# Two weight loads moved ahead of a branch, and a decode moved one step later, in a routed expert and gated block on one core

## The chip, the cores and the metric

The kernel runs on one core of a Trainium2 chip. The metric is the device time of one execution in microseconds, taken as the median of three runs. The profile is one execution of the same program, recorded by the hardware profiler; its rows count time from the first instruction.

## The reference

Linear attention, a routed expert layer and a gated linear block follow one another. All data is float32, but the weights of the gated block and of the router may arrive as 64-bit words, which the kernel decodes itself.

```python
kv  = einsum('bhsd,bhse->bhde', k, v)                 # 8 x 8 heads, 576 tokens, 64 wide
out = einsum('bhsd,bhde->bhse', q, kv)
x   = out / rms(out) * g_norm                         # 4608 tokens x 512
e   = argmax(x @ w_gate + modality_bias[modality_id]) # one of 8 experts
x   = gate_w * (relu(x @ w1[e]) @ w2[e])              # 512 -> 1024 -> 512, per token's expert
y   = (sigmoid(x @ wg) * (x @ wv)) @ wo               # 512 -> 1536 -> 512
```

## The kernel before

Every product is made of bfloat-like halves: an operand is split by ScalarE (ACT) into a rounded high part, and by VectorE (DVE) into the rest, and TensorE (PE) makes three matmuls of the halves. All order is written out by hand; each engine runs its instructions in the order of the program. The sync engine (SP) issues nearly all transfers, from one queue that runs in order: an instruction that has to wait holds all behind it.

The expert part handles 26 items, each in four steps. The last four sure items (`NSURE - 4` on) also carry work for the gated block, placed by `later(q, do)` at step q of the last 16. They load and transpose the first block of 512 tokens, load the weight rows of steps 0 and 1 of the gated block (`rows[0]`, `rows[1]`, 128 x 4 x 256 each, 512 KB) at q = 2, and split them: `split0` reads `rows[0]` at q = 8 and 10, `split1` reads `rows[1]` at q = 13 and 14 and stores the halves to `wt_d`. Then step 0 of the gated block is computed (`gv_first`), and a branch follows (`tc.If`): the items that are only sometimes needed are skipped or run.

Behind the branch the gated block runs over 5 blocks of tokens (the first of 512, the others of 1024) times 12 columns of 128 of the inner width: steps s = 1 to 59 (`NU` = 60). Steps 1 to 11 belong to the first block (`glu_plain`): 12 matmuls for the gate, then 12 of the output product of the step before, then 12 for the value. While PE does these, `prepare(s, spot)` is called at eight spots, in the order 0, 1, 6, 7, 2, 5, 4, 3, where 0 stands before the first product and 2 to 3 behind the second.

- Spot 0 issues loads: the output rows `wo` (`load_raw`, L922), `load_rows(s + 2)` (L1290) into `rows[s % 2]`, and a raw unit (`decode_late`, L1646).
- Spots 1 and 2 split the rows of step s + 1 (`group`: ACT L972, DVE L973); spot 2 also stores the halves (L1316).
- Spot 4 splits the output rows of step s + 1 (L1345, L1346) and the product of step s (L1350, L1351), which DVE has just multiplied (L996); it also scales the tokens of the next block by their gate (`weigh_y`, ACT L942, with factors that an indirect load fetches, L938) where a table (`TURNS`) says so.
- Spot 3 transposes such tokens on PE (L947), copies them out, and decodes a raw unit (`decode_late2`).

A unit is a 128 x 512 block of a weight, 512 KB as 64-bit words. Of 36 units 28 are decoded in the expert part. The last eight (`Late`, units 0 to 7) are decoded in the gated block: one ACT instruction (L1651), five DVE instructions (L1655 to L1661), and a store of 256 KB to `w_d` (L155 for units 0 to 3, L157 for units 4 to 7). Units 0 to 3 are the last four blocks of the value weight, which the rows of steps 8 to 11 need; units 4 to 7 are the output rows of steps 8 to 11. Two raw buffers alternate. Before, units 0 and 1 are loaded ahead of step 1, unit s in step s (2 to 7), and unit s - 1 is decoded at the end of step s (1 to 8). The tile `late` that holds them is handed on by `hold_y` at step 9, for split tokens of the next block.

Of the kernel before, what the change touches and what calls it, by code (L numbers as in the profile page):

```python
# [84 lines left out]
def attention_moe_glu_kernel(  # L85
# [4 lines left out]
    nc = tc.nc  # L90
# [825 lines left out]
    rows = [y0p.tile([128, 4, 256], F32, name=f"rows{i}") for i in range(2)]  # L916
# [3 lines left out]
    def load_raw(s, k):  # L920
        raw_o[s, 0] = (y0p if k % 2 == 0 else late_pool[0]).tile([128, DM], F32, tag="wo", name="wo", bufs=1)
        nc.sync.dma_start(out=raw_o[s, 0], in_=w_d[k // 4][:, k % 4, 1024:1536])  # L922
# [44 lines left out]
    def w_rows(j):  # L967
        return w_d[j // 4][:, j % 4, 0:1024].rearrange("p (k f) -> p k f", f=256)

    def split_w2(src, dst):  # L970

        nc.scalar.activation(out=dst[:, :, 0, :], in_=src, func=ACTF.Copy)  # L972
        nc.vector.tensor_tensor(out=dst[:, :, 1, :], in0=src, in1=dst[:, :, 0, :], op=ALU.subtract)  # L973
# [74 lines left out]
    with ExitStack() as st:  # L1048
# [12 lines left out]
        jobs = {}  # L1061
# [27 lines left out]
        def later(q, do):  # L1089
            tail.setdefault((NSURE - 4 + q // NJ1, q % NJ1), []).append(do)  # L1090
# [14 lines left out]
        def split0(g):  # L1105
            wt_first.append(dec.tile([128, 2, 2, 256], F32R, tag="d_raw", name="d_raw", bufs=4))
            split_w2(rows[0][:, 2 * g:2 * g + 2], wt_first[g])
            if g == 0:
                nc.sync.dma_start(out=wt_d[0][:, 0:2], in_=wt_first[0].bitcast(F32))
            else:  # L1110
                nc.sync.dma_start(out=wt_d[0][:, 2:3], in_=wt_first[1][:, 0:1].bitcast(F32))

        def split1(g):
            if g == 0:
                wts.append(grp.tile([128, 7, 2, 256], F32R, name="wt1"))
            split_w2(rows[1][:, 2 * g:2 * g + 2], wts[0][:, 2 * g:2 * g + 2])
            if g:
                nc.sync.dma_start(out=wt_d[1][:, 0:3], in_=wts[0][:, 0:3].bitcast(F32))
# [10 lines left out]
        for g in range(2):  # L1129
            later(8 + 2 * g, lambda g=g: split0(g))  # L1130
            later(13 + g, lambda g=g: split1(g))

        def gv_first(at):
            bank = lambda n: (phh.tile([128, 512], F32, tag="ph", name="ph") if n == "a" else
                              ptx.tile([128, 512], F32, tag="xt", name="xtp"))
            tmp = lambda n: xp.tile([128, XW], F32, tag="xg", name="xg", bufs=4)[:, 0:HC]
            glu_plain(lambda k: wt_first[k // 2][:, k % 2], y_of0, bank, tmp, lambda h: gm0, at)
# [73 lines left out]
    with ExitStack() as st:  # L1211
# [76 lines left out]
        def load_rows(s):  # L1288
            if s < 2 * NJ:
                nc.sync.dma_start(out=rows[s % 2], in_=w_rows(s % NJ))  # L1290

        def load_wt(s):
            if NJ <= s < NU:
                n = 3 if s < 2 * NJ else 7
                for lo, hi in ((0, 1), (1, n)):
                    nc.sync.dma_start(out=wts[s % 2][:, lo:hi].bitcast(F32), in_=wt_d[s % NJ][:, lo:hi])
# [3 lines left out]
        def sum_w(s):  # L1300


            if NJ <= s < 2 * NJ:
                r = rows[s % 2]
                t = wsum[s] = ws.tile([128, 4, 256], F32, tag="wsum", name="wsum", bufs=1)
                add = lambda o, a, c, op: nc.vector.tensor_tensor(out=o, in0=a, in1=c, op=op)
                add(t[:, 0], r[:, 3], r[:, 2], ALU.add)
                add(t[:, 1], t[:, 0], r[:, 0], ALU.subtract)
                add(t[:, 2], r[:, 0], r[:, 3], ALU.subtract)
                add(t[:, 3], r[:, 1], t[:, 1], ALU.subtract)  # L1310

        def group(s, g):
            if s < NJ:
                split_w2(rows[s % 2][:, 2 * g:2 * g + 2], wts[s % 2][:, 2 * g:2 * g + 2])
                if g:
                    nc.sync.dma_start(out=wt_d[s][:, 0:3], in_=wts[s % 2][:, 0:3].bitcast(F32))  # L1316
            elif s < 2 * NJ:
                a = 3 + 2 * g
                split_w2(wsum[s][:, 2 * g:2 * g + 2], wts[s % 2][:, a:a + 2])
                if g:  # L1320
                    nc.sync.dma_start(out=wt_d[s % NJ][:, 3:7], in_=wts[s % 2][:, 3:7].bitcast(F32))
# [6 lines left out]
        def load_o(s, z):  # L1328
            if (s, z) not in step_at:
                return  # L1330
            b, h, k = step_at[s, z]
            if b:
                split_o[s, z] = new_wos()
                nc.sync.dma_start(out=split_o[s, z].bitcast(F32), in_=wo_d[k][:, :, :])

        def ready_o(s, z):


            if (s, z) not in step_at:
                return  # L1340
            b, h, k = step_at[s, z]
            if b == 0:
                src = raw_o.pop((s, z))
                t = split_o[s, z] = new_wos()
                nc.scalar.activation(out=t[:, 0], in_=src, func=ACTF.Copy)  # L1345
                nc.vector.tensor_tensor(out=t[:, 1], in0=src, in1=t[:, 0], op=ALU.subtract)  # L1346
                nc.sync.dma_start(out=wo_d[k][:, :, :], in_=t.bitcast(F32))
            src = gms.pop((12 * b + k, h))
            hi, lo = (ws.tile([128, HC], F32R, tag=t, name=t, bufs=3) for t in ("gh", "gl"))
            nc.scalar.activation(out=hi, in_=src, func=ACTF.Copy)  # L1350
            nc.vector.tensor_tensor(out=lo, in0=src, in1=hi, op=ALU.subtract)  # L1351
            split_g[s, z] = (hi, lo)
            free_g.append(src)
# [261 lines left out]
        def number_y(b, i):  # L1615
            number(b, i, yr[i])
# [17 lines left out]
        jobs = {}  # L1634
# [27 lines left out]

        def decode_late(s):

            for i in ((0, 1) if s == 0 else (s,) if 1 < s < 8 else ()):
                jobs[i] = Late(units[NEARLY + i], i)

        def decode_late2(s):
            if 1 <= s < 9:
                d = jobs.pop(s - 1)  # L1670
                d.exponent()
                d.words()
                d.finish()
                d.store()

        def prepare(s, spot):


            b, j = divmod(s, NJ)
            if spot == 0:  # L1680
                load_wt(s + 1)
                if s + 2 <= NJ:
                    load_raw(s + 2, s + 1)
                load_rows(s + 2)
                decode_late(s)
                sum_w(s + 1)
            if spot == 6:
                ready_o(s, 1)
                load_o(s + 1, 0)
                load_o(s + 1, 1)  # L1690
            if spot == 1:
                group(s + 1, 0)
            if spot == 7:
                out_step((s, 0))
            if spot == 2:
                group(s + 1, 1)
            if spot == 4:
                ready_o(s + 1, 0)
                out_step((s, 1))
            if s > OPEN:  # L1700
                chunk_step(s, spot)
            if b + 1 < NB:
                for what, do in TURNS[min(b, 1)].get((j, spot), ()):
                    what(b + 1, do)
                if s == 9 and spot == 0:
                    hold_y(mw[1].tile([128, 2, 2, 2, HC], F32R, tag="w2r1", name="w2r1"))
                if s == 11 and spot == 3:
                    hold_y(yA[0][:, 0:2])
                if b and j == NJ - 1 and spot:
                    free_y.append(Y.pop((b, spot)))  # L1710
                for what in YPLAN[min(b, 2)].get((j, spot), ""):
                    y_step(b + 1, what)
            if b > 1:
                for what in YPLAN[min(b - 1, 2)].get((j + NJ, spot), ""):
                    y_step(b, what)
            if spot == 3:
                decode_late2(s)
            sums_o(s, spot)
            if (s, spot) == (FIRST, 0):
                yslots.extend(xp.tile([128, XW], F32, tag="xg", name="yr", bufs=4) for _ in range(2))  # L1720
                free_g.extend(xp.tile([128, XW], F32, tag="xg", name="yr", bufs=4)[:, 0:HC] for _ in range(2))
            if s == NU - 1 and spot in SPOTS[1:7]:
                last_load(SPOTS.index(spot) - 1)
            if (s, spot) == (OPEN, 3):
                open_chunks()
                chunk_step(s, spot)
# [2 lines left out]
        tmp = lambda n: ws.tile([128, HC], F32, tag=n, name=n, bufs=1)  # L1729
        late_pool.append(ws)  # L1730
        load_raw(2, 1)
        load_rows(2)
        for i in range(4):
            load_y(1, i)
        for i in range(4):
            number_y(1, i)
        decode_late(0)
        ready_o(1, 0)
        hold_y(yA[0], 2)
        hold_y(mw[1].tile([128, 2, 2, 2, HC], F32R, tag="w1r1", name="w1r1"))  # L1740
# [47 lines left out]
```

## Time and profile before

| | |
|---|---|
| median of 3 runs | 1472.84 us (1471.26 to 1475.34) |
| the profiled execution | 1472.33 us, of which its span (first to last instruction) 1470.5 us |
| granted TensorE clock, mean | 0.992 of full speed |
| busy, share of the span | PE 96%, DVE 69%, ACT 46%, POOL 18% |
| moved by DMA | 365.34 MB, mean 248 GB/s |

A busy share is the time in which the engine executes anything. PE's busy time counts pipelined matmuls whose ends are modelled, so 96% is not 96% of its peak. The clock column of the windows shows which of its two levels PE was granted: 1.00 is 2.4 GHz, 0.50 is 1.2 GHz.

### The profile page before, as it was taken

How to read it: one execution, taken by the hardware profiler on the slowest of the kernel's cores; microseconds unless marked ns; L12 is line 12 of the kernel's file. 1: busy time of each engine (PE TensorE's matmuls, PEld its weight loads, DVE VectorE, ACT ScalarE, POOL GpSimd, SP SyncE). 2: the span in 40 equal slices, each digit the busy share in tenths (PEclk: the TensorE clock that was granted, in tenths of full speed). 3: DMA queues.
4: the chain of work that ended last, by engine and by line, in shares of the span. 5: the costliest groups of instructions: out<-in, count | busy, mean ns of one | idle time of the engine just before them, and what ended most of it. 6: DMA issues, size and time to landing. Idle time of an engine off the chain costs nothing.

```text
span 1470.5 us, 24842 instructions
## 1 busy us (share of the span) xinstructions
PE 1417.6 (96%) x9302; PEld 1240.9 (84%) x9302; DVE 1009.5 (69%) x1592; ACT 677.6 (46%) x1080; POOL 269.7 (18%) x356
## 2 busy tenths in 40 slices
PE   6997999999999999989999999999999999999996
PEld 6886789999999998778888887888889888898896
DVE  1567868888888877647866676565876468655574
ACT  3676555556555556746433342332433235222241
POOL 1021122223121213111011101011024200131025
PEclk9999999999999999999999999999999999999999
DMA  9987599998985857689887656886666655565553
GB/s 297 332 302 248 184 318 309 267 327 284 302 287 187 289 164 241 235 273 335 317 337 255 243 194 248 327 285 232 208 215 221 207 203 186 196 215 199 193 162 111
DMA packets 189708, 365.34 MB, mean 248 GB/s; under 512 B 22544, under 2 KB 114448, under 8 KB 182416
## 3 DMA queue, kind: packets, MB, share of 16 engines
q1 hardware_dynamic: 177408, 330.37, 66.8%
q0 software_dynamic: 10816, 32.08, 6.0%
q8 instruction: 75, 1.23, 0.3%
q10 hardware_dynamic: 1360, 1.26, 0.3%
q14 instruction: 49, 0.40, 0.1%
HBM read 301.31 MB, written 74.93 MB: 256 GB/s over the span
## 4 chain that ended last, share of the span: by engine, by line
PE 52%; DMA 2%; DVE 1%; POOL 1%; issue 1%; ACT 0%; SPq 0%; another core or an unknown queue 0%; POOLq 0%; ACTq 0%; DVEq 0%
PE gv L1010 10%; PE gv L1011 10%; PE gv L1012 10%; PE ac L1490 4%; PE ac L1488 3%; PE ac L1489 3%; PE ac L1382 2%; PE ac L1383 2%; PE ac L1384 2%; PE gv L984 1%; PE gv L986 1%; PE gv L985 1%; PE tr L947 1%; DMA wos<-wp_d 1%; DMA rows<-w_d 1%
## 5 line engine op out<-in xcount | busy, mean ns | idle before, releaser
L279 PE MATMUL ph<-xh,w1h 128*128 128x256 f32 x576 | 167.2, 290 | 1.1 <-ACT w1h L235 1.1
L280 PE MATMUL ph<-xh,w1l 128*128 128x256 f32 x576 | 163.5, 284 | 0.9 <-DVE w1l L237 0.9
L281 PE MATMUL ph<-xl,w1h 128*128 128x256 f32 x576 | 163.5, 284 | 0.0
L1014 DVE TENSOR_TENSOR u<-u,gv 128x512 f32<-128x512 f32 x144 | 98.5, 684 | 78.5 <-PE gv L1012 77.8
L1488 PE MATMUL ac<-wos,gh 128*128 128x256 f32 x480 | 135.7, 283 | 2.3 <-ACT gh L1457 1.1
L1490 PE MATMUL ac<-wos,gl 128*128 128x256 f32 x480 | 136.3, 284 | 1.4 <-DVE gl L1450 1.3
L1489 PE MATMUL ac<-wos,gh 128*128 128x256 f32 x480 | 135.9, 283 | 0.0
L1010 PE MATMUL gv<-half,wt 128*128 128x512 f32 x336 | 132.2, 393 | 0.0
L1011 PE MATMUL gv<-half,wt 128*128 128x512 f32 x336 | 131.3, 391 | 0.0
L1012 PE MATMUL gv<-half,wt 128*128 128x512 f32 x336 | 131.0, 390 | 0.0
L279 PEld LDWEIGHTS ph<-xh,w1h 128*128 128x128 f32 x576 | 110.8, 192 | 3.0 <-ACT w1h L235 1.3
L280 PEld LDWEIGHTS ph<-xh,w1l 128*128 128x128 f32 x576 | 110.9, 193 | 2.8 <-DVE w1l L237 1.1
L281 PEld LDWEIGHTS ph<-xl,w1h 128*128 128x128 f32 x576 | 110.6, 192 | 0.0
L335 PE MATMUL py<-w2h,hh 128*128 128x512 f32 x272 | 106.9, 393 | 0.0
L336 PE MATMUL py<-w2l,hh 128*128 128x512 f32 x272 | 106.8, 393 | 0.0
L337 PE MATMUL py<-w2h,hl 128*128 128x512 f32 x272 | 106.0, 390 | 0.0
L1488 PEld LDWEIGHTS ac<-wos,gh 128*128 128x128 f32 x480 | 91.8, 191 | 7.2 <-issue 1.4
L1489 PEld LDWEIGHTS ac<-wos,gh 128*128 128x128 f32 x480 | 91.8, 191 | 3.7
L1490 PEld LDWEIGHTS ac<-wos,gl 128*128 128x128 f32 x480 | 91.8, 191 | 1.9 <-DVE gl L1450 1.8
L349 POOL DMA_INDIRECT y_d<-y,sidx x36 | 40.4, 1122 | 283.2 <-ACT y L345 110.5
L1043 ACT ACTIVATE u<-u 128x512 f32<-128x512 f32 x48 | 30.4, 633 | 134.1 <-DVE u L1014 134.1
L301 ACT ACTIVATE hh<-ph 128x512 fp32r<-128x512 f32 x68 | 40.6, 598 | 105.5 <-PE ph L281 105.5
(408 smaller groups left out, 3736.1 us busy)
## 6 DMA issues: line engine op xcount, KB each, us to landing
wt<-wt_d SPq DMA_DIRECT2D x36, 1536.0 KB
half<-in_moe_w_dram SPq DMA_DIRECT2D x96, 512.0 KB
w1r<-in_moe_w_dram SPq DMA_DIRECT2D x40, 512.0 KB
w2r<-in_moe_w_dram SPq DMA_DIRECT2D x40, 512.0 KB
wos<-wp_d SPq DMA_DIRECT2D x72, 256.0 KB
rows<-w_d SPq DMA_DIRECT2D x24, 512.0 KB
wt<-wt_d SPq DMA_DIRECT2D x48, 256.0 KB
wt_d<-wt SPq DMA_DIRECT2D x12, 1024.0 KB
```

Source lines behind the costliest of these rows:

```text
L279: nc.tensor.matmul(out=o, lhsT=bh[:, c, cs], rhs=hi[:, c, 0:n], start=(c == 0), stop=False)
L280: nc.tensor.matmul(out=o, lhsT=bl[:, c, cs], rhs=hi[:, c, 0:n], start=False, stop=False)
L281: nc.tensor.matmul(out=o, lhsT=bh[:, c, cs], rhs=lo[:, c, 0:n], start=False, stop=(c == KC - 1))
L335: nc.tensor.matmul(out=o, lhsT=hi[:, f, cs], rhs=bh[:, f, :], start=first, stop=False)
L336: nc.tensor.matmul(out=o, lhsT=hi[:, f, cs], rhs=bl[:, f, :], start=False, stop=False)
L337: nc.tensor.matmul(out=o, lhsT=lo[:, f, cs], rhs=bh[:, f, :], start=False, stop=last)
L1010: nc.tensor.matmul(out=o, lhsT=wh, rhs=yh[:, c, :], start=first and c == 0, stop=False, skip_group_check=True)
L1011: nc.tensor.matmul(out=o, lhsT=wh, rhs=yl[:, c, :], start=False, stop=False, skip_group_check=True)
L1012: nc.tensor.matmul(out=o, lhsT=wl, rhs=yh[:, c, :], start=False, stop=last and c == 1, skip_group_check=True)
L1488: nc.tensor.matmul(out=o, lhsT=gh[:, cs], rhs=wh, start=fresh and i % 2 == 0, stop=False, skip_group_check=True)
L1489: nc.tensor.matmul(out=o, lhsT=gh[:, cs], rhs=wl, start=False, stop=False, skip_group_check=True)
L1490: nc.tensor.matmul(out=o, lhsT=gl[:, cs], rhs=wh, start=False, stop=stop, skip_group_check=True)
```

## The change

Four places change. The rows of steps 2 and 3 are loaded ahead of the branch, at q = 12 and q = 15, into the buffers that the splits of steps 0 and 1 have read; the loads of the same rows behind the branch go away. Raw units 0 and 1 are loaded in spot 0 of step 1 instead of ahead of it, that is behind the tokens, the output rows of step 3 and the first store of output halves; unit s - 1 is loaded in step s (3 to 8). Each unit is decoded one step later (steps 2 to 9), and the tile is handed on at step 10.

```diff
@@ expert part, the last 16 steps
         for g in range(2):
             later(8 + 2 * g, lambda g=g: split0(g))
             later(13 + g, lambda g=g: split1(g))
+            later(12 + 3 * g, lambda g=g: nc.sync.dma_start(out=rows[g], in_=w_rows(2 + g)))
@@ gated block
         def decode_late(s):
-            for i in ((0, 1) if s == 0 else (s,) if 1 < s < 8 else ()):
+            for i in ((0, 1) if s == 1 else (s - 1,) if 2 < s < 9 else ()):
                 jobs[i] = Late(units[NEARLY + i], i)
         def decode_late2(s):
-            if 1 <= s < 9:
-                d = jobs.pop(s - 1)
+            if 2 <= s < 10:
+                d = jobs.pop(s - 2)
                 d.exponent()
                 d.words()
                 d.finish()
                 d.store()
@@ prepare, spot 0
                 load_wt(s + 1)
                 if s + 2 <= NJ:
                     load_raw(s + 2, s + 1)
-                load_rows(s + 2)
+                if s > 1:
+                    load_rows(s + 2)
                 decode_late(s)
                 sum_w(s + 1)
@@ prepare
-                if s == 9 and spot == 0:
+                if s == 10 and spot == 0:
                     hold_y(mw[1].tile([128, 2, 2, 2, HC], F32R, tag="w2r1", name="w2r1"))
@@ ahead of step 1
         load_raw(2, 1)
-        load_rows(2)
         for i in range(4):
             load_y(1, i)
         for i in range(4):
             number_y(1, i)
-        decode_late(0)
         ready_o(1, 0)
```

## Rows read from the trace of the kernel before

**Rows 1.** Chain that ended last, behind the branch: start us, us, what.

```profile
637.08 9.04 DMA rows<-w_d
646.21 0.64 ACT wt L972
...
647.48 0.69 DVE gm L996
...
648.73 0.71 ACT yr L942
649.49 1.97 PE tr L947 x8
651.46 0.43 PE gv L984
...
660.25 0.87 PE tr L947 x8
```

**Rows 2.** Waits of PE, 615 to 725 us: total, times, longest us.

```profile
PE tr L947 <- ACT yr L942: 3.8, 1, 3.8
```

**Rows 3.** Windows of PE: us, busy (count), granted clock, DMA share, GB/s.

```profile
53.00:54.00 1.00, 0.72 (x18) 1.00 1.04 389
...
650.00:651.00 1.00, 1.00 (x6) 0.50 0.90 252
...
653.00:654.00 1.00, 1.00 (x6) 1.00 1.01 422
```

**Rows 4.** Timeline of PE near 53 us: start, us, what, idle before.

```profile
53.28 0.73 PE L479 MATMUL kv<-vt,kt 64*64 64x64 f32 x17 [2.70 <-issue]
```

**Rows 5.** Timeline of the SP queue, behind the branch: when a transfer was issued.

```profile
630.15 0.42 SPq L1290 DMA_DIRECT2D rows<-w_d  x1
...
685.04 0.32 SPq L157 DMA_DIRECT2D w_d<-w2r  x1
...
685.89 0.44 SPq L1290 DMA_DIRECT2D rows<-w_d  x1
...
694.09 0.32 SPq L157 DMA_DIRECT2D w_d<-w2r  x1
...
694.94 0.44 SPq L1290 DMA_DIRECT2D rows<-w_d  x1
```

**Rows 6.** Timeline of ACT: its waits for rows in steps 1, 7 and 8.

```profile
634.60 1.15 ACT L972 ACTIVATE wt<-rows 128x512 fp32r<-128x512 f32 x2 [1.89 <-DMA rows<-w_d]
...
692.48 1.15 ACT L972 ACTIVATE wt<-rows 128x512 fp32r<-128x512 f32 x2 [1.60 <-DMA rows<-w_d]
...
701.76 1.16 ACT L972 ACTIVATE wt<-rows 128x512 fp32r<-128x512 f32 x2 [2.78 <-DMA rows<-w_d]
```

**Rows 7.** Timeline of PE: last product of step 2, first of steps 8 and 9.

```profile
645.29 0.39 PE L986 MATMUL gv<-half,wt 128*128 128x512 f32 x1
...
695.40 0.39 PE L984 MATMUL gv<-half,wt 128*128 128x512 f32 x1
...
703.56 0.39 PE L984 MATMUL gv<-half,wt 128*128 128x512 f32 x1
```

**Rows 8.** DMA issues of the page: count, KB each, median us to landing.

```profile
y_d<-y POOLq DMA_DIRECT2D x4, 264.0 KB, 3.5
```

**Rows 9.** Chain that ended last, near the end of the span.

```profile
1424.68 4.41 DMA wos<-wp_d
```

**Rows 10.** Waits of the SP queue, 575 to 725 us.

```profile
SPq L157 <- DVE w2r L1661: 18.7, 4, 5.2
...
SPq L1099 <- DMA y_d<-y,sidx: 8.9, 1, 8.9
```

**Rows 11.** Windows of all engines, shortly before the branch.

```profile
616.00:620.00 4.00, 4.00 (x24) 2.84 (x23) 3.83 (x6) 3.16 (x6) 0.00 (x0) 1.00 0.00 0
```

**Rows 12.** The tile of the scale factors, 635 to 650 us.

```profile
L938 POOL DMA_INDIRECT gate_t<-gate_d,oid x4: 963/980/1376, 636.9 to 641.8; - x4
...
DMA to landing us min/median/max: 5.7/5.8/6.6
```

## The prediction

> **What bounds the kernel now.** I read the page's shares first, then the waits of the matrix engine (PE) around the branch, the chain of waits there, the PE clock, and last the timelines of the sync engine's DMA queue, of ScalarE (ACT) and of PE. PE is busy 96% of the span, so only an idle PE counts, and an edit off PE is worth what it gives or takes there. The table of PE's waits from 615 to 725 us, which holds the end of the expert part, the branch and steps 1 to 11 of the last part, has one wait of size: 3.8 us in which transposes wait for a scaling pass on ACT [rows 2]. PE passes the branch itself almost without a pause. In the chain [rows 1] the reader sees why: the rows load that is issued at 637.08 lands 9.04 us later; only then can ACT split it (646.21); the vector multiply of step 2 (VectorE, DVE) stands behind a split too and starts at 647.48; ACT's split of that product and its scaling of `yr` (648.73) follow; PE starts at 649.49. PE's last product before began at 645.29 and took 0.39 [rows 7], so the idle time is 645.68 to 649.49, 3.81 us. After it the granted clock is 0.50 (1.2 GHz) until it is back at 1.00 (2.4 GHz) by 653 [rows 3]: eight transposes take 1.97 instead of 0.87, and three products 0.43 each instead of 0.23 [rows 1], 1.10 + 0.60 = 1.7 us. So rows that come late cost 5.5 us, 0.37% of the time. That is all the change can win here.
>
> **The change, part by part: the two early rows.** Two rows loads (steps 2 and 3, 512 KB each) leave the queue behind the branch and go before it. No instruction is added. The cover: from 616 to 620, shortly before the branch, the DMA share is 0.00 [rows 11]. The first load goes out when the splits of step 0's rows have freed its buffer, the second behind the store of step 1's split, the last thing that the queue issues before the branch. A 512 KB load needed 4.4 us behind the branch (issued 630.15, ACT released at 634.60, [rows 5, 6]) and at worst 9.04 [rows 1]; the rows are first split in steps 1 and 2, behind the branch, so I cost the two loads at nothing. Were that cover gone, they would cost what they do now.
>
> **Where that stall goes.** With the rows there, ACT and DVE have no split left to do when PE ends step 2. What is late next is a chain of engines that the edit does not touch: multiply on DVE, then ACT's split of it, then ACT's scaling, then PE. From 647.48 to 649.49 that chain takes 2.01 [rows 1]; with 0.05 for the first hand-over PE still idles 2.06. ACT works in program order, so the scaling can't pass the split. The scale factors come by indirect DMA: the four are issued from 636.9 to 641.8 and land 5.7 to 6.6 us later [rows 12]; the two that count are the first two, the second of them issued a third of the way, near 638.5, and in place by 645.1, before ACT comes to them at 647. The gap shrinks by 3.81 - 2.06 = 1.75. Does the clock hold through 2.06 us? An idle time of 2.70 us at 53.28 [rows 4] left it at 1.00 [rows 3], so I take the 1.7 as won too: gain 3.4. Ends: 1.7 (the clock falls all the same) and 5.5 (no gap at all).
>
> **The raw units one step later.** Eight raw loads, eight decodes (one ACT, five DVE instructions) and eight stores remain, each one step later. Early, this only empties the queue: step 1 loads two raw units behind its own inputs, step 2 loads none and stores none. The price is at the other end. The store of a decoded unit is issued as the last act of a step's vector work; the queue waits for it (18.7 us in 4 waits, [rows 10]). Before, every load that reads a decoded piece came a step after its store. Now it comes right behind it: in step 6 the rows of step 8 need unit 3, in steps 7 to 10 the wo load needs units 4 to 7. Such a load can't be issued until the store has landed, and the queue runs in order, so the rows load behind it, the raw load and the stores wait too. That a queue stands still for a landing store is seen elsewhere: 8.9 us for a `y_d` store [rows 10].
>
> Cost of one such wait. Let W be the time from the store's issue to its landing, R that of the rows load. For step 7: the store goes at 694.09 [rows 5], then W, 0.45 for the wo load's issue, R, then the ACT split (0.64) and the DVE one (0.69, as the passes in [rows 1]), and PE wants the result at 703.56 when step 9 starts [rows 7]. Room: 703.56 - 694.09 - 0.45 - 1.33 = 7.69 for W + R. For step 6, whose wo load needs no wait: 695.40 - 685.04 - 1.33 = 9.03.
> W is not in the trace of before. Nearest rows: 3.5 for a 264 KB store from another queue [rows 8], and 4.41 for a 256 KB load on this one [rows 9]; the upper bound is what a rows load takes in the same traffic, 6.8 (694.94 to 701.76, [rows 5, 6]). I take 4.4, nearest in size and queue. R is at least 4.4 (at 630.15, little in front) and at most 6.8; step 6 shows 6.6 (685.89 to 692.48). While the queue waits nothing new is issued, so the traffic in front is smaller than now, but a raw load and two stores follow at once: I take 5.0, near the quiet end. W + R = 9.4, 1.7 over the room of step 7 and 0.4 over that of step 6. Each load serves the step after next, so two chains alternate: step 9 starts 1.7 late, step 11 another 1.7; the chain through steps 8 and 10 gives 0.4 + 1.7, less than the other and covered by it. Sum 3.4. Behind step 10's wait stands the first load of the next phase's weights (step 12); no row says if it is late: between 0 and another 1.7, I take 0.4, as two steps lie between. Loss 3.8. By the lower ends (7.9) it is 2 x 0.2 = 0.4, by the upper ends (13.6) 2 x 5.9 = 11.8.
>
> The Trainium skill (DMA: Bandwidth & Descriptors, section Anatomy of one DMA) says that a DMA engine never waits for a semaphore, the issuing sequencer does; that is the mechanism which speaks against this edit, and the 8.9 us agree. It also gives a fixed cost of some 2.0 us, mostly the write's receipt, plus bytes at 436 GB/s: an estimate of 2.6 for W and 3.2 for R, together 5.8. By it no step is late and the loss is nothing; the measured 3.5 and 4.4 are longer.
>
> The buffer that is handed over at step 10 instead of 9 is first written by an ACT split at the start of step 11. It may wait for the last store by some 2 us; ACT then still does its step-11 sigmoid well before the multiply at that step's end needs it. Cost nothing; without that cover, those 2 us.
>
> **Sum.** -3.4 + 3.8 = +0.4 on the profiled execution's 1472.33 (span 1470.5): 1472.7. The median of the three runs is 0.51 above that execution: 1473.2.
>
> **Rivals.**
> No late step: W + R fits in 7.7. Then only the gain remains, -3.4: 1469.4. For it: the lower ends miss by 0.2 only, and the queue is drained while it waits. Against: ACT already waits 1.60 and 2.78 us for rows [rows 6]. The Trainium skill's figures, by the estimate above, give this case too.
> Slower: the store waits behind a full queue. One mechanism: each step's raw load and two stores go out just before the next decode's store, so W becomes 5.0 (the 4.4 and 0.6 of the traffic in front) and R its worst, 6.8. W + R = 11.8, 4.1 over; twice is 8.2, and one of those idle times, over 3.8, costs the clock again, 1.7. +9.9 - 3.4 = +6.5: 1479.3. It decides from W + R of about 11.6 without a clock fall (2 x 3.9 = 7.8 = 3.4 + 4.4). For it: 6.6 and 6.8 are what R is now. Against: the queue stands empty part of the time.
> Gap wholly gone and no loss: -5.5, 1467.3. For it: the whole idle time is laid to the rows load. Against: the 2.01 us chain of three engines.
> The gap stays because a scale factor or the wo load is late instead: 0 + 3.8, 1476.6. Against: both land before 646 by the rows.
>
> **Chances and range.** Forecast 0.42, no late step 0.22, slower 0.24, gap gone 0.09, gap stays 0.03. Faster or slower by over 0.3% (4.4 us, about what a measurement of this kernel can tell) are only "gap gone", 0.09, and "slower", 0.24; the rest is 0.67. The range goes from just under the no-late-step case to just over the slower one, 1468.9 to 1480: it leaves out the gap-gone case and the worst of W + R. The forecast's own range is 1470 to 1476.
>
> **What would show it.** Right: PE's wait near 645 is about 2 us, and the clock stays at 1.00 at 650; ACT's splits of steps 2 and 3 wait for no DMA; waits of the queue for a `w_d` store appear in steps 6 to 10, 3.5 to 6 us each; PE idles 1 to 2 us at steps 9 and 11. Wrong: no such PE waits between 690 and 730 (then 1469), or PE waits of 3 us and more with the clock at 0.50 after them (then 1479).

## The result, and the profile after

The changed kernel takes 1484.54 us (median of 5; 1481.37 to 1490.22) against 1472.82 (median of 5): ratio 1.0076, 95% interval 1.0061 to 1.0092. It is 11.7 us slower, and 4.5 us above the top of the predicted range.

The profiled execution is the slowest of the five (1490.22 us, span 1488.4), 17.9 us longer than the one shown of before. PE's first product of step 1 starts at 633.42 instead of 629.11, its first of step 12 at 743.16 instead of 728.04. So 4.3 us were lost ahead of the branch, 10.8 between steps 1 and 12 (109.74 us instead of 98.93), and 2.8 behind. The 4.3 are not the change. PE is already 4.3 us later than before at 215 us, some 390 us ahead of the first instruction that moved; and two kernels below whose code is the same up to the branch, rows_alone and rows_weigh, start step 1 at 633.37 and 627.70. Windows of PE in this execution (us, busy, granted clock, DMA share, GB/s) show half clock in work that is the same in both kernels; the execution of before has 1.00 in all three.

```profile
52.00:56.00 4.00, 3.47 (x28) 0.60 1.07 371
93.00:97.00 4.00, 4.00 (x96) 0.60 1.09 358
196.00:199.00 3.00, 2.51 (x11) 0.53 1.05 382
```

Where PE waits, 600 to 780 us, answering to [rows 2]:

```profile
PE gv L984 <- ACT wt L972: 4.6, 2, 3.6
PE gv L1010 <- DMA wt<-wt_d: 2.9, 1, 2.9
PE tr L947 <- ACT yr L942: 2.1, 1, 2.1
```

The old wait is down from 3.8 to 2.1, and two kinds are new: products that wait for split rows, and the first product of the next phase that waits for its weights. PE's timeline (start, us, idle before) gives their places: behind step 2, then steps 9, 10 and 12.

```profile
652.04 1.27 PE L947 MATMUL tr<-ident,yr 128*128 128x128 f32 x8 [2.05 <-ACT yr L942]
...
707.65 0.50 PE L984 MATMUL gv<-half,wt 128*128 128x512 f32 x1 [1.00 <-ACT wt L972]
...
719.93 0.80 PE L984 MATMUL gv<-half,wt 128*128 128x512 f32 x1 [3.56 <-ACT wt L972]
...
743.16 0.79 PE L1010 MATMUL gv<-half,wt 128*128 128x512 f32 x1 [2.92 <-DMA wt<-wt_d]
```

Behind three of the four the granted clock is at its lower level (windows of PE, compare [rows 3]):

```profile
654.00:655.00 1.00, 1.00 (x4) 0.50 0.98 404
...
720.00:722.00 2.00, 2.00 (x5) 0.50 1.00 416
...
746.00:748.00 2.00, 2.00 (x6) 0.50 0.96 389
```

What the products wait for is seen on ACT, whose waits for rows grew from the 1.60 and 2.78 of [rows 6]:

```profile
696.48 1.16 ACT L972 ACTIVATE wt<-rows 128x512 fp32r<-128x512 f32 x2 [2.69 <-DMA rows<-w_d]
...
706.97 1.15 ACT L972 ACTIVATE wt<-rows 128x512 fp32r<-128x512 f32 x2 [5.06 <-DMA rows<-w_d]
...
719.25 1.15 ACT L972 ACTIVATE wt<-rows 128x512 fp32r<-128x512 f32 x2 [7.62 <-DMA rows<-w_d]
```

And what the rows wait for is on the SP queue. Its table of waits, 575 to 740 us, has two rows that before does not have:

```profile
SPq L922 <- DMA w_d<-w2r: 24.5, 4, 7.4
...
SPq L1291 <- DMA w_d<-w2r: 2.7, 1, 2.7
```

Five times the queue stands still until a store of a decoded unit has landed. The SP timeline of steps 7 to 9 (when each transfer was issued) answers to [rows 5]:

```profile
697.02 0.32 SPq L157 DMA_DIRECT2D w_d<-w2r  x1
701.99 0.32 SPq L922 DMA_DIRECT2D wo<-w_d  x1
702.36 0.42 SPq L1291 DMA_DIRECT2D rows<-w_d  x1
702.88 0.38 SPq L1647 DMA_DIRECT2D w2r<-in_moe_w_out_dram  x1
703.35 0.38 SPq L1317 DMA_DIRECT2D wt_d<-wt  x1
703.83 0.51 SPq L1348 DMA_DIRECT2D wo_d<-wos  x1
705.16 0.32 SPq L157 DMA_DIRECT2D w_d<-w2r  x1
712.98 0.32 SPq L922 DMA_DIRECT2D wo<-w_d  x1
713.35 1.50 SPq L1291 DMA_DIRECT2D rows<-w_d  x1
...
716.37 0.83 SPq L157 DMA_DIRECT2D w_d<-w2r  x1
724.44 0.32 SPq L922 DMA_DIRECT2D wo<-w_d  x1
724.80 0.43 SPq L1291 DMA_DIRECT2D rows<-w_d  x1
```

From a store (L157) to the wo load that reads what it wrote (L922) there are 4.97, 7.82 and 8.07 us; in before there are 0.4 (694.09 to 694.50). Read the six lines from 701.99 to 705.16: once released, the queue sends off in 3 us all that it had held back, 2.6 MB in five transfers (256, 512, 512, 768 and 512 KB), and the next store follows straight behind them. From 702 to 713 us, between the release and the landing of that next store, the windows show 262 GB/s, 2.88 MB: the five transfers and the store's own 0.26 MB. So the store landed when all that was sent off ahead of it had been moved.

### The profile page after: what moved, and what is told of

Same layout as the page of the kernel before. It is cut to its first block, busy times and chain, and to the rows that moved or that the text cites. A ratio compares the mean times of both kernels' runs of the same rounds, so it can differ in the third digit from the quotient of the medians.

```text
span 1488.4 us, 24842 instructions
## 1 busy us (share of the span) xinstructions
PE 1430.7 (96%) x9302; PEld 1249.4 (84%) x9302; DVE 1010.0 (68%) x1592; ACT 677.0 (45%) x1080; POOL 272.4 (18%) x356
## 4 chain that ended last, share of the span: by engine, by line
PE 50%; DMA 3%; DVE 2%; issue 1%; POOL 1%; ACT 1%; SPq 0%; POOLq 0%; ACTq 0%; DVEq 0%
PE gv L1010 10%; PE gv L1011 10%; PE gv L1012 10%; PE ac L1491 4%; PE ac L1490 3%; PE ac L1489 3%; PE ac L1383 2%; PE ac L1384 2%; PE ac L1385 2%; DMA w_d<-w2r 1%; PE tr L947 1%; PE gv L984 1%; PE gv L986 1%; PE gv L985 1%; DMA wos<-wp_d 1%
## 5 line engine op out<-in xcount | busy, mean ns | idle before, releaser
L349 POOL DMA_INDIRECT y_d<-y,sidx x36 | 43.6, 1212 | 281.7 <-ACT y L345 95.8
```

## The experiments

Theory A: the early rows gain about what was forecast; all of the loss is the wait of the queue behind a store, because the decode now ends right ahead of the loads that read it. Rivals: the early loads disturb something (B), the moved traffic or the later decode work is itself too much, or the clock alone.

All ratios are against before. The third column is the time from PE's first product of step 1 to its first of step 12 in the profiled execution, which leaves out what happens ahead of the branch; the fourth, PE's idle times over 0.3 us in that stretch, each with the step that it precedes.

| kernel | ratio, 95% interval | steps 1 to 12, us | PE idle, us (step) |
|---|---|---|---|
| before | 1 | 98.93 | 3.81 (3) |
| changed | 1.0076 [1.0061, 1.0092] | 109.74 | 2.05 (3), 1.00 (9), 3.56 (10), 2.92 (12) |
| rows_alone | 0.9991 [0.9980, 1.0001] | 96.62 | 2.06 (3), 0.42 (7) |
| decode_alone | 1.0062 [1.0045, 1.0080] | 107.54 | 2.05 (3), 4.63 (10), 2.55 (12) |
| no_read_wait | 0.9992 [0.9979, 1.0005] | 97.08 | 2.05 (3), 0.64 (12) |
| early_wait | 1.0036 [1.0019, 1.0052] | 103.51 | 2.48 (3), 4.06 (10) |
| rows_first | 1.0015 [1.0004, 1.0027] | 101.71 | 2.05 (3), 2.67 (12) |
| no_raw | 1.0029 [1.0015, 1.0042] | 102.29 | 2.05 (3), 0.33 (10), 0.32 (11), 2.44 (12) |
| free_ten | 1.0012 [1.0000, 1.0025] | 99.57 | 2.06 (3), 2.24 (12) |
| rows_weigh | 0.9977 [0.9967, 0.9987] | 95.30 | 0.74 (4), 0.41 (7) |
| weigh_first | 0.9966 [0.9953, 0.9979] | 93.63 | none |

**rows_alone: only the early rows.** The edits of `decode_late`, `decode_late2` and `hold_y` are undone:

```diff
+            later(12 + 3 * g, lambda g=g: nc.sync.dma_start(out=rows[g], in_=w_rows(2 + g)))
...
+                if s > 1:
+                    load_rows(s + 2)
...
-        load_rows(2)
```

> The rows of steps 2 and 3 are loaded ahead of the branch, the decode stays as it was. Theory A (the early rows gain a little, the late decode costs all): PE's wait at the end of step 2 falls from 3.8 to 2.05 us as in the changed kernel, and no PE wait appears in steps 8 to 12. If the clock falls after those 2.05 us the gain is 1.8 us, if it holds 3.4: ratio 0.9977 to 0.9988. Theory B (the early loads themselves disturb the branch or the transfers behind it and cost a good part of the 11.7 us): slower, ratio 1.003 or more, with PE waits between 690 and 750 us.

PE's timeline behind step 2, and the windows at the place where the changed kernel has half clock:

```profile
652.00 1.27 PE L947 MATMUL tr<-ident,yr 128*128 128x128 f32 x8 [2.06 <-ACT yr L942]
```

```profile
653.00:654.00 1.00, 1.00 (x7) 1.00 1.13 287
654.00:655.00 1.00, 1.00 (x6) 1.00 0.81 168
```

The idle time is 2.06 and the clock held. The stretch is 2.3 us shorter, the median 1.9 us lower: 0.9991, a little above the range that theory A gave, with an interval that just reaches 1. By the end of step 3 PE is 3.0 us ahead of before; 0.7 are lost again at step 7, where transposes wait 0.42 us for ACT's scaling, which before does not show (that pass starts at 687.88, when the scale factor issued at 680.4 has just landed, 6.3 to 7.4 us from the issue). No PE wait appears in steps 8 to 12. Theory B, which asked for 1.003, falls.

**decode_alone: only the later decode.**

```diff
-            for i in ((0, 1) if s == 0 else (s,) if 1 < s < 8 else ()):
+            for i in ((0, 1) if s == 1 else (s - 1,) if 2 < s < 9 else ()):
...
-            if 1 <= s < 9:
-                d = jobs.pop(s - 1)
+            if 2 <= s < 10:
+                d = jobs.pop(s - 2)
```

> The raw units are loaded and decoded one step later, the rows of steps 2 and 3 stay behind the branch. Theory A: the queue waits for stores of decoded units 4 to 8 us in each of steps 6 to 10, PE idles at steps 9, 10 and 12 by some 7 us with clock falls of 3.4 us behind two of them; the rows of step 3 land earlier than before, since two raw loads no longer stand ahead of them, so the wait in step 2 shrinks to between 2.05 and 3.8. Ratio 1.006 to 1.009. Theory B: no slower than before, within 0.3%.

Its SP waits show the same two rows as the changed kernel, the first of them thus:

```profile
SPq L922 <- DMA w_d<-w2r: 23.8, 4, 8.4
```

The loss is there without the early rows: +8.6 us in the stretch, with PE idle at steps 10 and 12; at step 9, where it was also expected, PE does not idle over 0.3 us. PE's wait behind step 2 is 2.05 here as well. Two raw loads fewer in front of step 3's rows are enough for that; the early loads were not needed for it.

**no_read_wait: the changed kernel without the waits behind stores.** The wo loads of steps 8 to 11's output rows and the rows load of step 8 read a part of `w_d` written long ago:

```diff
-        nc.sync.dma_start(out=raw_o[s, 0], in_=w_d[k // 4][:, k % 4, 1024:1536])
+        nc.sync.dma_start(out=raw_o[s, 0], in_=w_d[min(k // 4, 1)][:, k % 4, 1024:1536])
...
-                nc.sync.dma_start(out=rows[s % 2], in_=w_rows(s % NJ))
+                nc.sync.dma_start(out=rows[s % 2], in_=w_rows(4 if s == 8 else s % NJ))
```

> The changed kernel, but the output rows of steps 8 to 11 and the weight rows of step 8 are read from a part of the decoded weights that has long been written (other data, the same bytes and queue order), so that no load waits for the store right ahead of it. Theory A: the queue's waits for stores of decoded units go away, so do PE's waits of 1.0, 3.6 and 2.9 us and the clock falls behind them; what is left is the gain of the early rows, ratio 0.9977 to 0.9990. Rival (the moved traffic itself is too much for steps 6 to 11, whoever waits): the PE waits stay, ratio 1.005 or more.

On its SP timeline the wo load follows its store at once, as in before:

```profile
703.42 0.32 SPq L157 DMA_DIRECT2D w_d<-w2r  x1
703.79 0.42 SPq L922 DMA_DIRECT2D wo<-w_d  x1
```

Bytes, order and the later decode are those of the changed kernel, and 12.7 of its 109.74 us go: PE waits at steps 9 and 10 are absent. Of the one at step 12, 0.64 us stays:

```profile
730.36 0.50 PE L1010 MATMUL gv<-half,wt 128*128 128x512 f32 x1 [0.64 <-DMA wt<-wt_d]
```

Of the 12.7 us 1.6 are the clock in step 3 and not the waits: it fell behind step 2 in the changed kernel (step 3 took 10.70 us) and held here (9.10). The other 11 us are the waits behind stores, and what the later bytes cost by themselves is small: the 0.64 us at step 12, and a stretch 0.5 us longer than that of rows_alone. The ratio 0.9992 lies just above the range expected, 0.9977 to 0.9990.

**early_wait: the converse.** rows_alone with the old decode, and a wait put in: in steps 7 to 9 the wo load reads the unit that has just been stored.

```diff
-        nc.sync.dma_start(out=raw_o[s, 0], in_=w_d[k // 4][:, k % 4, 1024:1536])
+        nc.sync.dma_start(out=raw_o[s, 0], in_=w_d[k // 4][:, min(k % 4 + (k > 7), 3), 1024:1536])
```

> rows_alone with the decode on its old schedule, but in steps 7 to 9 the wo load reads the unit whose store stands right ahead of it in the queue (other data, the same bytes). So the wait is added without the later decode. Theory A (the wait behind the store is the cost): the queue waits 4 to 8 us in each of the three steps, ACT's waits for rows grow by as much, PE idles at steps 9 to 11 or 12; three waits in place of five: 3 to 9 us over rows_alone, ratio 1.001 to 1.005. Rival (it is the later decode itself on ACT and DVE that delays the steps): as rows_alone, ratio 0.998 to 1.000, no PE wait between 690 and 750 us.

```profile
703.89 0.32 SPq L157 DMA_DIRECT2D w_d<-w2r  x1
710.41 0.32 SPq L922 DMA_DIRECT2D wo<-w_d  x1
```

These SP lines of step 8 show 6.5 us. Three such waits add 6.9 us to rows_alone's stretch (103.51 against 96.62), with one PE wait of 4.06 at step 10. The later decode is not needed for such a loss: the wait alone makes one.

**rows_first: the rows ahead of the wait.**

```diff
+                if s > 1:
+                    load_rows(s + 2)
                 if s + 2 <= NJ:
                     load_raw(s + 2, s + 1)
-                if s > 1:
-                    load_rows(s + 2)
```

> The changed kernel with the two loads of spot 0 swapped: the weight rows are issued ahead of the output rows, so that in steps 7 to 10 the rows pass before the queue waits for the store; only step 6 still makes the rows wait. Theory A in the form that the rows behind the wait are what is late: PE's waits at steps 9 and 10 go, the queue's waits stay (some 3.5 to 8 us in four steps, now with the rows' 512 KB ahead of them or not); the wait at step 12 for the next phase's weights is 0 to 1 us. Ratio 0.998 to 1.001. If instead everything behind the wait counts (raw unit, stores, output rows), half of the loss stays: ratio 1.003 or more.

The waits of the queue stay (SP timeline, step 9):

```profile
707.62 0.32 SPq L157 DMA_DIRECT2D w_d<-w2r  x1
707.99 1.28 SPq L1291 DMA_DIRECT2D rows<-w_d  x1
714.88 0.32 SPq L922 DMA_DIRECT2D wo<-w_d  x1
```

7.26 us, but the rows are off by then, and PE does not wait at steps 9 and 10. What is left is 2.67 us at step 12, more than the 0 to 1 that I expected. The ratio 1.0015 lies just over the top of that expectation and below the 1.003 of its rival. Of the stretch, 1.6 us are again half clock in step 3 (10.67 us).

**no_raw: less in front of the store.** The changed kernel without three of the raw loads:

```diff
-                nc.sync.dma_start(out=self.raw, in_=src)
+                if i < 5:
+                    nc.sync.dma_start(out=self.raw, in_=src)
```

> The changed kernel without the loads of raw units 5, 6 and 7 (their decodes run on what the buffers hold). This takes 512 KB out of what the queue issues in steps 6, 7 and 8 just ahead of the next store. If the store's long landing (4.9, 7.8 and 8.1 us in steps 7, 8 and 9 of the changed kernel, where 4.4 was taken) comes from the transfers in front of it, it falls by about 1.4 us (512 KB at some 370 GB/s) in steps 7, 8 and 9, and PE's waits of 3.6 and 2.9 us shrink or go: ratio 1.000 to 1.005. If it is the store's own time, the landings stay and the ratio is that of the changed kernel, 1.0076.

```profile
692.86 0.32 SPq L157 DMA_DIRECT2D w_d<-w2r  x1
695.81 0.32 SPq L922 DMA_DIRECT2D wo<-w_d  x1
...
701.00 0.32 SPq L157 DMA_DIRECT2D w_d<-w2r  x1
704.55 0.32 SPq L922 DMA_DIRECT2D wo<-w_d  x1
...
709.16 0.32 SPq L157 DMA_DIRECT2D w_d<-w2r  x1
714.71 0.32 SPq L922 DMA_DIRECT2D wo<-w_d  x1
```

Steps 7, 8 and 9: 2.95, 3.55 and 5.55 us where the changed kernel has 4.97, 7.82 and 8.07. Executions of the same code differ here too: up to step 9 rows_first and free_ten are the same, and their times from store to load are 2.66 and 3.72 us in step 6 and 5.06 and 6.23 in step 8, and no further apart in steps 7 and 9. The falls of 2.0, 4.3 and 2.5 are beyond that spread of 1.2. So the store's landing follows what was issued ahead of it, by more than the 1.4 us of one transfer's bytes; that a wait which ends earlier also leaves less of a backlog for the next would explain the rest, but was not tried by itself. PE's waits at steps 9 and 10 go but for 0.33 and 0.32 us at steps 10 and 11; the one at step 12 stays.

**free_ten: is it step 10's wait that makes step 12 late?** rows_first, with step 10's wo load reading what was written a step earlier:

```diff
-        nc.sync.dma_start(out=raw_o[s, 0], in_=w_d[k // 4][:, k % 4, 1024:1536])
+        nc.sync.dma_start(out=raw_o[s, 0], in_=w_d[k // 4][:, 2 if k == 11 else k % 4, 1024:1536])
```

> rows_first, but the output rows that step 10 loads are read from a place that was written a step earlier (other data, the same bytes), so that the queue has no store to wait for in step 10; the waits in steps 7 to 9 stay. If PE's wait of 2.7 us at step 12, and the clock fall behind it, come from the wait in step 10 alone, which holds back the first load of the next phase's weights, they go: 2.7 to 4.4 us under rows_first, ratio 0.998 to 1.000. If the earlier waits have already made the queue that late, the wait at step 12 stays at 2 us or more and the ratio at rows_first's 1.0015.

The second case came: the wait of step 10 alone is not the reason. It is gone (3 waits behind stores at the wo loads instead of 4), yet PE still waits 2.24 us at step 12:

```profile
725.79 2.50 SPq L1297 DMA_DIRECT2D wt<-wt_d  x2
```

```profile
733.51 0.50 PE L1010 MATMUL gv<-half,wt 128*128 128x512 f32 x1 [2.24 <-DMA wt<-wt_d]
```

The load goes out 7.7 us ahead of PE's product and is late; in before it goes out at 722.49, 5.6 us ahead of the product at 728.04, and is in time. Without its wait PE would have begun step 12 at 731.27, 5.5 us behind the issue. So here the load is not issued late, it takes longer. Which transfers in front of it do that was not tried. (The stretch is 2.1 us shorter than that of rows_first; 1.6 of that is the clock, which held in step 3 here.)

**rows_weigh and weigh_first: can the rest of the first wait be had?** rows_weigh is rows_alone with the first two tiles scaled ahead of ACT's split of the product; weigh_first adds the swap of rows_first, on the old decode, where no store is waited for:

```diff
-            for at, what in plan + [((p + 2 + p // 2, 2 if p else 4), weigh_y), ...
+            for at, what in plan + [((p + 2 + p // 2, 2), weigh_y), ...
```

> As rows_alone, and the first two tiles of the next block are scaled at spot 2 of step 2, ahead of ACT's split of the step's product, not at spot 4 behind it. If the 2.05 us that are left of the wait are the chain multiply, split, scale, then PE's wait at the end of step 2 goes to under 0.5 us and the clock stays at full: 5.0 to 5.6 us in all, ratio 0.9962 to 0.9967. If the scale factors land too late for it (they land some 6 us after their issue), the wait only moves: 1 to 2 us left, ratio as rows_alone.

> rows_weigh (early rows, old decode, the scaling ahead of the split) with the rows issued ahead of the output rows in spot 0. In rows_weigh ACT still waits 3.7 us for the rows of step 5, which leaves PE 0.74 us idle at the transposes behind step 3. The rows go out some 0.6 us earlier and have 256 KB less in front: that idle time shrinks to 0 to 0.3 us, 0.5 us gained: ratio 0.9970 to 0.9977. If the output rows become late instead, no gain: 0.9977 or more.

ACT in rows_weigh, steps 2 and 3: the scale factors come 0.45 us late for the second tile, which PE does not feel; the rows of step 5 come 3.67 late, which it does.

```profile
643.11 0.72 ACT L942 ACTIVATE yr<-yr,gate_t 128x512 f32<-128x512 f32 x1 [0.45 <-DMA gate_t<-gate_d,oid]
...
652.30 1.15 ACT L972 ACTIVATE wt<-rows 128x512 fp32r<-128x512 f32 x2 [3.67 <-DMA rows<-w_d]
```

The transposes behind step 2 follow the products without a wait (PE's timeline):

```profile
644.12 1.04 PE L947 MATMUL tr<-ident,yr 128*128 128x128 f32 x8
```

The gain is 3.9 us by the medians (1468.94 against 1472.87), short of the 5.0 to 5.6 expected; PE is 4.8 us ahead at the start of step 3 and loses again at its two waits, the new one of 0.74 us ahead of step 4 and the 0.41 at step 7, which rows_alone has too. In weigh_first ACT's wait is halved and PE does not wait at all between steps 1 and 12:

```profile
653.10 1.15 ACT L972 ACTIVATE wt<-rows 128x512 fp32r<-128x512 f32 x2 [1.82 <-DMA rows<-w_d]
```

Its stretch is 5.3 us shorter than that of before. It takes 1466.68 us against 1472.57, ratio 0.9966, a little below the 0.9970 to 0.9977 expected: it beats both kernels.

## Why the prediction was wrong

**The early rows cost nothing: right in the main.** rows_alone has one new PE wait, 0.42 us at step 7, and its queue waits for no store of a decoded unit. The buffer handed on a step later cost nothing either: ACT waits 0.31 us for the last store (at 734.06), PE does not.

**2.06 us of the wait are left: right,** to 0.01 us, in seven of the kernels; early_wait has 2.48. rows_weigh shows that the chain multiply, split, scale was the reason.

**The clock holds through them, gain 3.4: half right.** It held in rows_alone, where this place gained 3.0 us, and fell in the changed kernel after the same idle time, where it gained 1.4 (2.4 behind step 2, less 0.9 in step 3), below the lower end of 1.7. The forecast rested on one idle time of 2.70 us in one execution [rows 4]. In the changed kernel's own profile PE idles 2.31 us at that same place, ahead of 52.53, and the windows above show 0.60 behind it. What a row shows of the clock once is no promise for the next execution.

**The decode one step later makes the queue wait behind stores, and the rows behind those waits come late: the mechanism was right.** decode_alone, no_read_wait and early_wait show it from three sides. The places were not all right: steps 9 and 11 were forecast late, and steps 9, 10 and 12 were. The chain through step 10, which the forecast took as covered by the other, has the longest wait.

**W = 4.4 is the step that failed.** Measured from the store to the load behind it: 3.96 in step 6 (687.96 to 691.92), then 4.97, 7.82, 8.07 and 5.72. Only the first of these is as short as forecast, and two pass even the upper bound of 6.8. R was right: 4.6 to 5.9, where 5.0 was taken. I took W from a load near the end of the span [rows 9], where the DMA share is 0.59 (1424 to 1429 us), and let only R grow with the traffic. That a standing queue thins the traffic held for R, but for W the opposite counts: the wait gathers the next transfers into a burst, and the next store, whose time DVE sets, goes out behind it. no_raw and the 2.88 MB show the dependence. The slower rival had this mechanism, but it gave the extra time to R and took W = 5.0. With the measured 7.82 and 5.9, W + R in step 8 is 6.0 over the room of 7.69, not 1.7.

PE's wait there is 3.56 and not 6.0, for two reasons. Measured from the store, PE itself came 1.7 us later to step 10 than in before, for the most part because it had already waited at step 9. And the room was counted 0.65 too small: PE starts 0.68 us behind ACT's pass (719.25 to 719.93), not 1.33 behind both passes. For step 7 the sum came out near by luck: W was 0.57 longer and R 0.39 shorter than forecast, 9.58 against 9.4, and with the room counted too small PE's wait was 1.00 and not 1.7.

The Trainium skill (DMA: Bandwidth & Descriptors, section Anatomy of one DMA) gives by an estimate 2.6 for W and 3.2 for R, from a fit of DMAs that GpSimd issues; both are below all that these runs show on the busy queue, and the case without late steps, which it stood for, did not come.

**No clock loss behind the late steps: wrong.** After the 3.56 and the 2.92 us PE runs at the lower level. In the chain of the changed kernel the wait for the weights is followed by products that are 0.43 apart for over 5 us, where 0.23 is normal:

```profile
735.85 7.27 DMA wt<-wt_d
743.16 0.79 PE gv L1010
743.95 0.43 PE gv L1011
...
748.64 0.43 PE gv L1010
```

The forecast held no such term, only the slower rival had one.

**0.4 at step 12: wrong,** 2.92. no_read_wait leaves 0.64 of it, so the rest comes from the waits, but not from the wait in step 10 alone: free_ten, without it, still has 2.24.

**The sum.** In the profiled execution, step by step against before: -2.4 behind step 2, +0.9 in step 3 (half clock), +1.2, +4.1, +2.6 and +4.3 in steps 8 to 11 (the last with the wait for step 12), 10.8 in all, and 2.8 behind, where the half clock lasts. By the medians 11.7. Forecast: -3.4 + 3.8. So the gain fell short by 2.0, and the late steps cost 12.2, or 15.0 with what is behind, in place of 3.8.

## What to carry to other kernels

Here a load that reads what a store on the same in-order queue has just written cost the store's landing, and that landing included all that the queue had let off ahead of it; once a wait had made a burst, the next store paid for it. Look for a step of distance between such a store and its reader (before has it, and does not wait), or put what is urgent ahead of the pair (rows_first, which took the loss from 1.0076 to 1.0015). When a wait is traced to one late transfer, look at what is next in the chain behind it: here the transfer was worth 1.8 us of PE time, and the order of two ACT instructions the other 2.

## What the runs showed of the hardware

The same idle time of 2.05 us of PE was followed by half clock in the changed kernel and in rows_first, and not in rows_alone, decode_alone, no_read_wait, no_raw or free_ten, although free_ten has the code of rows_first up to step 9. What decides it was not found. Executions of the same code differ by such spells elsewhere too: the first 200 us of the changed kernel's profile have three that the profile of before does not have, and by 215 us it is the 4.3 us late that step 1 then starts late. rows_alone and rows_weigh, the same code up to the branch, start step 1 5.7 us apart. A stretch between two marks of the trace tells more here than the span.

The queue's waits leave the DMA engines idle and then flood them: the DMA share is 0.10 from 712 to 713 us, as a store lands and the queue is released, and 1.02 from 708 to 709, while the burst of the wait before is being moved.
